# A new hand-written order for the first 26 slots of a linear attention with two feed-forward layers

## The chip, the cores and the metric

The kernel runs on one core of a Trainium2 chip. The core has five engines with an instruction list each: TensorE (PE, matrix products), VectorE (DVE), ScalarE (ACT), GpSimd (POOL) and SyncE (SP, which issues almost all transfers here). Each works its list strictly in order and waits at an instruction until what it needs is there. The metric is the device time of one execution in microseconds; the number quoted is the median of several runs.

## The reference

For 4 batches, 8 heads, 768 steps and head size 48, a state of 48 x 48 per head is carried along the steps; the result then goes through two feed-forward layers of width 2048 over 3072 tokens of 384 features.

```python
for t in range(S):
    cur = einsum('bhd,bhe->bhde', u[None] * k_t, v_t)
    y[:, :, t] = einsum('bhd,bhde->bhe', r_t, state + cur)
    state = w[None, :, :, None] * state + einsum('bhd,bhe->bhde', k_t, v_t)
h = x @ w_in1;  x = (max(h, 0) + alpha * min(h, 0)) @ w_out1
h = x @ w_in2;  x = (h * tanh(log1p(exp(h)))) @ w_out2
```

Weights are given as 64-bit floats, everything else as 32-bit floats.

## The kernel before

Tokens go in six blocks of 512 columns (128 steps of all four batches). A *slot* is one block with one of the 16 groups of 128 hidden features: slots 0 to 95 are the first layer (`mA_...`), and the second layer (`mB_...`) has as many behind them. Slot 2, slot 8 and so on below are first-layer slots of block 0 and block 1.

Every large product is taken as three with operands split in a high and a low part (`PASSES`), so a slot is nine products for `mA_h` (to the bank `h`, of which there are two in turn) and nine for `mA_out` (to the banks `acc`). Between them stand `mA_g` (ACT takes the negative part, DVE the weighted sum, L658 and L660), `mA_hi` (ACT) and `mA_lo` (DVE). Slots 0 and 1 are cut in halves of the columns and in passes: `mA_h 0 1 2` is slot 0, half 1, pass 2.

A weight group passes through `more_raw` (SP loads the raw words; three buffers in turn, a buffer is free again after that group's `w_join`), `w_scale` (ACT, two operations), `w_join` (DVE), `w_hi` (ACT) and `w_lo` (DVE). For groups 0 and 1 each of these is done in two halves.

Attention goes in *units*. Units 0 to 3 are the four batches' first 128 steps, each through `load_unit`, `m_first`, `prep_rk`, `c_first`, `preset_first`, `scores`, `masked`, `attend0`, `x_first`, `x_first_lo`, and then `prep_kn` and `states_first` for the state. Tables of decay powers (`tables`, `scale_Kn`, `table_Kn`, `seats`) and the constants `cst` (identity and mask) come before. From unit 4 on a unit is 64 steps of two batches: `load_unit`, `prep_pair`, `prep_c`, `prep_c2`, `prep_kn`, `preset`, `masked`, then `batch` (TensorE, which also holds the next unit's `scores` and takes one `h` bank), `t_decay`, `t_update`, and `x_parts`, which moves the result out of the banks and sets the `h` bank free.

The order is written out by hand. Each step has a name (its function and arguments) and `PLACES` gives the place at which it is issued; `run_plan` sorts all steps by place and issues them, so a step's place sets its order on every engine it uses, SP included. A step with the place `None` is left out. An entry `"?name": 1` moves that step to another engine, by `other()`:

```python
def other():
    return PLACES.get("?" + now[0], 0)
```

For `w_hi` that is POOL instead of ACT, for `w_lo`, `prep_pair`, `prep_rk` and `m_first` POOL instead of DVE, for `preset` one POOL operation instead of four of ACT, for `prep_c2` sixteen short ACT operations instead of one reduction on DVE, for `t_decay` four ACT operations instead of one of DVE.

`keep_warm` multiplies zeros into a bank that nobody reads, to keep TensorE at work where it would wait: five groups ahead of all steps, and those that `PLACES` gives a place.

Of the kernel before, what the change touches and what calls it, by code (L numbers as in the profile page):

```python
# [54 lines left out]
def more_state(u):  # L55
# [9 lines left out]
    "?preset 9 1": 1, "tables": 8.049, "keep_warm 3#######": 8.099, "scale_Kn": 8.149, "memset": 8.199,  # L65
    "load_unit 0": 8.249, "m_first 0": 8.299, "prep_rk 0": 8.349, "c_first 0": 8.399, "pad_v 0": 8.449,
    "load_unit 1": 8.499, "preset_first 0": 8.549, "dma_start": 8.599, "table_Kn 1": 8.649, "pad_v 1": 8.699,
    "m_first 1": 8.749, "prep_rk 1": 8.799, "load_unit 3": 8.849, "<lambda> 3": 8.899, "load_unit 2": 8.949,
    "load_k 2": 8.999, "<lambda> 0": 9.049, "scores 0": 9.099, "masked 0": 9.149, "m_first 3": 9.199, "seats": 9.249,
# [24 lines left out]
    "w_join (0,7)": 15.199, "w_scale (0,8)": 15.249, "dma_start##": 15.299, "w_join (0,8)": 15.349, "mA_hi 3": 15.399,  # L94
# [1017 lines left out]
```

## Time and profile before

| | us |
|---|---|
| runs (median 863.0) | 862.88, 863.0, 864.82 |
| the profiled execution, its time | 864.74 |
| the profiled execution, its span | 862.8 |
| TensorE busy | 854.3 |
| DVE busy | 629.9 |
| ACT busy | 612.3 |
| POOL busy | 115.1 |

The span is the time from the first to the last instruction of the profiled execution; its own time is a little longer. Busy times of engines overlap. An engine's idle time matters only where another engine, in the end TensorE, waits for it.

### The profile page before, as it was taken

What the parts mean: (1) busy time and instruction counts of PE and PEld (TensorE: products, weight loads), DVE (VectorE), ACT (ScalarE), POOL (GpSimd) and SP (SyncE); (2) the same over time, 40 slices, a digit from 0 to 9 for tenths busy, and PEclk for the clock granted to TensorE, in tenths of its full rate; (3) what the DMA queues carried; (4) which work ended last, traced back from release to release, by engine and by line L of the source; (5) the groups of instructions that cost most, each with busy time, mean ns of one, the idle gap of its engine ahead of it and who ended that gap; (6) DMA issues with size and microseconds to landing.
All of it is one profiled execution on the core that took longest, in us unless ns stands there. A gap on an engine that the chain in (4) does not pass through costs nothing.

```text
span 862.8 us, 16681 instructions
## 1 busy us (share of the span) xinstructions
PE 854.3 (99%) x6382; PEld 709.8 (82%) x6382; DVE 629.9 (73%) x969; ACT 612.3 (71%) x1170; POOL 115.1 (13%) x133
## 2 busy tenths in 40 slices
PE   9999999999999999999999999999999999999998
PEld 6887888888888888888888888888888888888897
DVE  8889776666656656444666887887887887887875
ACT  5987555445545445543556989989989998998886
POOL 5465641112211112100002000000000000000000
PEclk9999999999999999999999999999999999999999
DMA  9886734364255434223520300110110110100101
GB/s 347 260 247 179 223 99 133 96 206 135 84 163 162 147 85 171 66 65 120 172 78 15 111 1 1 32 43 1 30 45 1 29 47 0 30 9 1 28 10 38
DMA packets 65328, 79.95 MB, mean 93 GB/s; under 512 B 39648, under 2 KB 52448, under 8 KB 65248
## 3 DMA queue, kind: packets, MB, share of 16 engines
q1 hardware_dynamic: 64688, 78.78, 30.4%
q8 instruction: 50, 0.82, 0.4%
q14 instruction: 30, 0.25, 0.1%
q10 hardware_dynamic: 560, 0.10, 0.1%
HBM read 61.16 MB, written 15.73 MB: 89 GB/s over the span
## 4 chain that ended last, share of the span: by engine, by line
PE 92%; DVE 2%; ACT 2%; DMA 2%; issue 1%; POOL 0%; SPq 0%; DVEq 0%; ACTq 0%; POOLq 0%
PE h L269 43%; PE acc L690 21%; PE sc L817 8%; PE acc L817 8%; PE yt L817 4%; PE acc L815 2%; PE sc L501 1%; DMA nat<-in_nat 1%; PE h L532 1%; PE sc L815 1%; PE yt L553 1%; PE sc L546 1%; DMA cst<-in_consts 1%; PE yt L532 1%; ACT wrawr L216 0%
## 5 line engine op out<-in xcount | busy, mean ns | idle before, releaser
L269 PE MATMUL h<-x,w 128*128 128x512 f32 (+1 forms) x1746 | 415.5, 387 | 2.1 <-DVE x L190 1.9
L269 PEld LDWEIGHTS h<-x,w 128*128 128x128 f32 x1746 | 325.0, 188 | 69.7 <-issue 2.5
L690 PE MATMUL acc<-ghi,w 128*128 128x512 f32 x516 | 174.9, 394 | 0.0
L658 ACT ACTIVATE m<-h 128x512 f32<-128x512 f32 x96 | 57.1, 595 | 92.8 <-PE h L269 92.7
L660 DVE SCALAR_TENSOR_TENSOR g<-m,oma,h 128x512 f32<-128x512 f32 x96 | 71.6, 746 | 60.2 <-ACT m L658 59.2
L690 PEld LDWEIGHTS acc<-ghi,w 128*128 128x128 f32 x516 | 96.8, 188 | 21.3
L187 ACT ACTIVATE ghi<-g 128x512 fp32r<-128x512 f32 x86 | 54.2, 630 | 74.9 <-PE acc L690 48.0
L690 PE MATMUL acc<-glo,w 128*128 128x512 f32 x258 | 100.4, 389 | 0.0
L190 DVE TENSOR_TENSOR glo<-g,ghi 128x512 fp32r<-128x512 f32 x86 | 62.8, 730 | 51.5 <-ACT ghi L187 51.2
L754 DVE SCALAR_TENSOR_TENSOR a<-ghi,h 128x512 f32<-128x512 f32 x96 | 66.0, 687 | 38.5 <-ACT ghi L751 32.0
L754 DVE SCALAR_TENSOR_TENSOR g<-s,c 128x512 f32<-128x512 f32 x95 | 66.6, 701 | 22.5 <-ACT s L751 20.4
L762 ACT ACTIVATE m<-h 128x512 f32<-128x512 f32 x96 | 56.4, 588 | 35.6 <-PE h L269 35.6
L190 DVE TENSOR_TENSOR gloB<-g,ghiB 128x512 fp32r<-128x512 f32 x105 | 72.0, 685 | 7.1 <-ACT ghiB L187 7.1
L751 ACT ACTIVATE ghi<-m,biases 128x512 f32<-128x512 f32 x96 | 69.6, 725 | 3.2
L187 ACT ACTIVATE ghiB<-g 128x512 fp32r<-128x512 f32 x105 | 64.8, 617 | 9.1 <-PE acc L690 6.9
L751 ACT ACTIVATE glo<-ghi,biases 128x512 f32<-128x512 f32 x96 | 68.1, 709 | 0.1
L751 ACT ACTIVATE s<-glo,biases 128x512 f32<-128x512 f32 x96 | 68.1, 709 | 0.0
L751 ACT ACTIVATE s<-s,biases 128x512 f32<-128x512 f32 x96 | 68.0, 708 | 0.0
L817 PE MATMUL sc<-ghiB,w 128*128 128x512 f32 x192 | 66.9, 389 | 0.0
L754 DVE SCALAR_TENSOR_TENSOR b<-ghi,a 128x512 f32<-128x512 f32 x96 | 65.6, 684 | 0.1
L754 DVE SCALAR_TENSOR_TENSOR c<-glo,b 128x512 f32<-128x512 f32 x95 | 65.7, 691 | 0.0
L817 PE MATMUL acc<-ghiB,w 128*128 128x512 f32 x192 | 61.7, 389 | 0.0
(189 smaller groups left out, 1148.3 us busy)
## 6 DMA issues: line engine op xcount, KB each, us to landing
wrawr<-in_w SPq DMA_DIRECT2D x28, 768.0 KB, 5.3
nat<-in_nat SPq DMA_DIRECT2D x40, 288.0 KB, 4.4
w2d<-wj SPq DMA_DIRECT2D x16, 384.0 KB, 2.5
wraw<-w2d SPq DMA_DIRECT2D x16, 384.0 KB, 3.1
rk<-in_rkT SPq DMA_DIRECT2D x40, 128.0 KB, 3.1
x2d<-xo SPq DMA_DIRECT2D x6, 768.0 KB, 3.2
x<-x2d SPq DMA_DIRECT2D x6, 768.0 KB, 4.6
rk<-in_rkT SPq DMA_DIRECT2D x40, 96.0 KB, 2.8
```

Source lines behind the costliest of these rows:

```text
L187: act.activation(out=hi, in_=src, func=AF.Copy)
L190: eng.tensor_tensor(out=lo, in0=src, in1=hi.bitcast(F32), op=ALU.subtract)
L269: pe.matmul(h[:, n], w_in(layer, f, a, c), x[:, b, c, n], start=(k == 0), stop=(k == 3 * KC - 1))
L532: pe.matmul(y[i][64 * q:64 * q + 64, p * HC:(p + 1) * HC], T[ROWS[h], 2 * bp + i, k, :], pair[i][ROWS[h], 0, k, t], start=(r == 0 and not ...
L658: act.activation(out=m, in_=hA[s], func=AF.Relu, scale=-1.0)
L660: dve.scalar_tensor_tensor(out=g, in0=m, scalar=oma[:, f:f + 1], in1=hA.pop(s), op0=ALU.mult, op1=ALU.add)
L690: pe.matmul(acc[0][c], w_out(0, f, a)[:, c * 128:(c + 1) * 128], g[b], start=(f == 0 and k == 0), stop=(f == NF - 1 and k == 2))
L751: act.activation(out=out, in_=in_, func=AF.Square, scale=scale, bias=fin[bias])
L754: dve.scalar_tensor_tensor(out=out, in0=in0, scalar=scalar, in1=in1, op0=op0, op1=ALU.mult)
L762: act.activation(out=bnew("t", n), in_=v["h", n], func=AF.Tanh, scale=0.5)
L815: pe.matmul(acc[1][t][:, :DM], g[a][:, t * C:(t + 1) * C], w_out(1, f, b), **se)
L817: pe.matmul(acc[1][t], w_out(1, f, a)[:, t * 128:(t + 1) * 128], g[b], **se)
```

## The change

Only `PLACES` is changed: the places of all steps up to 26.599, the set of steps that go to another engine, and one group of zero products more that gets no place. From `mA_hi 22` on the order is the same. The core of the diff, with the lines that matter below (each side is a dictionary in the order of places; lines left out hold the same steps at other places):

```diff
-    "?w_lo (0,4)": 1, "?t_decay 4": 1, "?t_decay 9": 1, "?preset_first 1": 1, "?prep_c2 4": 1, "?t_decay 5": 1,
-    "?preset 6 0": 1, "?w_lo (0,12)": 1, "?t_decay 6": 1, "?w_hi (0,15)": 1, "?preset 8 0": 1, "?preset 8 1": 1,
-    "?prep_pair 10 1": 1, "?preset 9 0": 1, "?w_hi (0,1) 1": 1, "?preset 4 0": 1, "?m_first 2": 1, "?w_hi (0,3)": 1,
-    "?w_hi (0,4)": 1, "?prep_pair 6 1": 1, "?prep_pair 8 1": 1, "?preset 7 0": 1, "?preset 7 1": 1, "?w_lo (0,15)": 1,
-    "?preset 9 1": 1, "tables": 8.049, "keep_warm 3#######": 8.099, "scale_Kn": 8.149, "memset": 8.199,
-    "load_unit 0": 8.249, "m_first 0": 8.299, "prep_rk 0": 8.349, "c_first 0": 8.399, "pad_v 0": 8.449,
-    "load_unit 1": 8.499, "preset_first 0": 8.549, "dma_start": 8.599, "table_Kn 1": 8.649, "pad_v 1": 8.699,
...
-    "prep_rk 2": 9.799, "prep_rk 3": 9.849, "keep_warm 3##########": 9.899, "load_k 1": 9.949, "scores 1": 9.999,
...
-    "w_scale (0,1) 0": 10.299, "keep_warm 3#########": 10.349, "w_join (0,0) 0": 10.399, "w_join (0,0) 1": 10.449,
...
-    "w_lo (0,8)": 16.249, "load_unit 5": 16.299, "prep_c 5": 16.349, "mA_h 6": 16.399, "w_hi (0,7)": 16.449,
...
-    "masked 4": 17.249, "mA_out 5": 17.299, "batch 4": 17.349, "mA_hi 6": 17.399, "mA_lo 6": 17.449, "mA_out 6": 17.499,
-    "prep_kn 5": 17.549, "w_scale (0,10)": 17.599, "load_unit 7": 17.649, "w_hi (0,9)": 17.699, "w_join (0,10)": 17.749,
-    "mA_h 8": 17.799, "mA_g 7": 17.849, "t_decay 4": 17.899, "w_lo (0,9)": 17.949, "mA_hi 7": 17.999, "mA_lo 7": 18.049,
-    "mA_out 7": 18.099, "prep_pair 6 0": 18.149, "x_parts 4": 18.199, "preset 5 0": 18.249, "preset 5 1": 18.299,
-    "masked 5": 18.349, "mA_g 8": 18.399, "w_hi (0,10)": 18.449, "t_update 4": 18.499, "w_scale (0,11)": 18.549,
...
+    "?w_lo (0,4)": 1, "?preset_first 1": 1, "?t_decay 5": 1, "?t_decay 6": 1, "?w_hi (0,15)": 1, "?preset 8 1": 1,
+    "?prep_pair 10 1": 1, "?w_lo (0,15)": 1, "?m_first 3": 1, "?w_lo (0,1) 1": 1, "?w_lo (0,1) 0": 1, "?w_hi (0,3)": 1,
+    "?preset 4 0": 1, "?w_hi (0,9)": 1, "?t_decay 4": 1, "?prep_c2 5": 1, "?preset 5 0": 1, "?preset 5 1": 1,
+    "?w_hi (0,10)": 1, "?w_hi (0,13)": 1, "?prep_c2 8": 1, "?prep_pair 10 0": 1, "?preset 10 0": 1, "tables": 8.099,
+    "load_unit 0": 8.149, "<lambda> 0": 8.199, "load_unit 3": 8.249, "m_first 0": 8.299, "scale_Kn": 8.349,
+    "prep_rk 0": 8.399, "c_first 0": 8.449, "preset_first 0": 8.499, "dma_start": 8.549, "table_Kn 1": 8.599,
+    "load_unit 1": 8.649, "m_first 1": 8.699, "scores 0": 8.749, "masked 0": 8.799, "dma_start#": 8.849,
+    "tensor_scalar": 8.899, "seats": 8.949, "pad_v 1": 8.999, "load_unit 2": 9.049, "<lambda> 2": 9.099,
...
+    "m_first 2": 9.449, "pad_v 2": 9.499, "more_raw 2": 9.549, "more_raw 1": 9.599, "keep_warm 3#######": 9.649,
...
+    "keep_warm 3##########": 10.449, "w_scale (0,1) 0": 10.499, "w_join (0,0) 0": 10.549, "w_join (0,0) 1": 10.599,
...
+    "mA_hi 0": 13.599, "w_hi (0,1) 1": 13.649, "more_raw 8": 13.699, "more_raw 9": 13.749, "mA_lo 0": 13.799,
...
+    "mA_hi 2": 14.599, "mA_lo 2": 14.649, "mA_h 3": 14.699, "prep_c 4": 14.749, "mA_g 3": 14.799, "load_unit 5": 14.849,
...
+    "mA_g 6": 17.149, "preset 4 1": 17.199, "masked 4": 17.249, "w_hi (0,8)": 17.299, "load_unit 7": 17.349,
+    "w_lo (0,8)": 17.399, "mA_hi 6": 17.449, "mA_lo 6": 17.499, "more_raw 15": 17.549, "more_raw 16": 17.599,
+    "mA_g 7": 17.649, "prep_kn 4": 17.699, "w_lo (0,9)": 17.749, "batch 4": 17.799, "x_parts 4": 17.849,
+    "prep_c 6": 17.899, "w_scale (0,10)": 17.949, "prep_pair 6 0": 17.999, "w_join (0,10)": 18.049,
+    "w_hi (0,10)": 18.099, "mA_hi 7": 18.149, "mA_lo 7": 18.199, "mA_h 8": 18.249, "mA_h 9": 18.299, "mA_g 8": 18.349,
+    "t_decay 4": 18.399, "t_update 4": 18.449, "prep_c2 6": 18.499, "preset 5 0": 18.549, "preset 5 1": 18.599,
+    "prep_kn 5": 18.649, "w_scale (0,11)": 18.699, "masked 5": 18.749, "mA_hi 8": 18.799, "mA_lo 8": 18.849,
...
```

On SP the loads go, before: unit 0, unit 1, `cst`, unit 3, unit 2, ..., weights 0 to 6, unit 4, weights 7 to 9, `ubt`, weight 10, unit 5, unit 6, weights 11 and 12, unit 7, ... After: unit 0, unit 3, `cst`, unit 1, `al`, unit 2, ..., weights 0 to 6, `ubt`, unit 4, weights 7 and 8, unit 5, weight 9, unit 6, weights 10 to 13, unit 7, weights 14 and 15, unit 8, ...

On TensorE, from slot 2 on, before: `mA_h 2`, `mA_out 0`, `mA_h 3`, `mA_out 1`, `mA_h 4`, `mA_h 5`, `mA_out 2`, `mA_out 3`, `mA_h 6`, `scores 4`, `mA_out 4`, `mA_h 7`, `mA_out 5`, `batch 4`, `mA_out 6`, `mA_h 8`, `mA_out 7`, and, behind `x_parts 4`, `mA_h 9` and on. After: `mA_h 2`, `mA_out 0`, `mA_h 3`, `mA_out 1`, `mA_h 4`, `mA_out 2`, `mA_out 3`, `mA_h 5`, `mA_h 6`, `mA_out 4`, `mA_h 7`, `scores 4`, `mA_out 5`, `batch 4`, `mA_h 8`, `mA_h 9`, `mA_out 6`, `mA_out 7`, `mA_out 8`, `mA_h 10`, `batch 5`, and on.

## Rows read from the trace of the kernel before

**Rows 1.** The page, part 1: busy us (share of the span) and instructions.

```profile
PE 854.3 (99%) x6382; PEld 709.8 (82%) x6382; DVE 629.9 (73%) x969; ACT 612.3 (71%) x1170; POOL 115.1 (13%) x133
```

**Rows 2.** Busy time by stretch: from:to, length, engines, granted clock, DMA share, GB/s.

```profile
8.54:31.31 22.77, 22.36 (x380) 19.48 (x380) 20.80 (x27) 19.51 (x49) 13.33 (x16) 1.00 0.96 362
31.31:67.97 36.66, 34.42 (x299) 27.55 (x296) 31.60 (x38) 31.25 (x74) 18.68 (x16) 1.00 0.85 245
67.97:95.00 27.03, 27.03 (x475) 22.31 (x476) 24.35 (x41) 20.20 (x46) 15.98 (x14) 1.00 0.69 206
95.00:220.00 125.00, 125.00 (x1383) 103.32 (x1382) 79.42 (x127) 61.75 (x151) 33.62 (x39) 1.00 0.47 138
220.00:858.00 638.00, 637.21 (x3826) 531.87 (x3825) 467.65 (x728) 476.83 (x847) 29.87 (x38) 1.00 0.20 58
```

**Rows 3.** Timeline of TensorE at 67.97: start us, us, instructions merged, [idle before <-releaser].

```profile
67.97 2.33 PE L269 MATMUL h<-x,w 128*128 128x512 f32 x9 [1.87 <-DVE x L190]
```

**Rows 4.** Timeline of TensorE: the first zero products, and `scores 4`.

```profile
1.30 6.08 PE L641 MATMUL acc<-ghi 128*128 128x384 f32 x12 [1.30 <-POOL ghi L943]
...
50.42 0.69 PE L501 MATMUL sc<-rk 48*64 48x64 f32 x32
```

**Rows 5.** The chain that ended last, in order of time: start us, us, what.

```profile
3.15 5.26 DMA cst<-in_consts
...
45.37 8.54 DMA nat<-in_nat
...
82.63 2.04 PE acc L690 x9
...
86.58 2.28 PE h L269 x9
```

**Rows 6.** Groups of DVE instructions, 30 to 68 us: count, busy us, mean ns, idle before.

```profile
L225 DVE SCALAR_TENSOR_TENSOR wj<-wrawr 128x768 uint32<-128x768 uint32 x7 | 7.9, 1136 | 0.8 <-ACT wrawr L217 0.7
L190 DVE TENSOR_TENSOR glo<-g,ghi 128x512 fp32r<-128x512 f32 x8 | 6.5, 819 | 2.3 <-ACT ghi L187 2.3
L190 DVE TENSOR_TENSOR w<-wj,w 128x768 fp32r<-128x768 f32 x6 | 6.1, 1043 | 0.0
L660 DVE SCALAR_TENSOR_TENSOR g<-m,oma,h 128x512 f32<-128x512 f32 x8 | 6.0, 744 | 1.6 <-ACT m L658 1.3
L419 DVE TENSOR_TENSOR rk<-rk,RKs 112x1024 f32<-112x1024 f32 x3 | 5.9, 1950 | 0.0
L505 DVE COPY_PREDICATED Ah<-cst,sc 128x512 f32<-128x512 uint32 x2 | 1.5, 737 | 0.0
L454 DVE TENSOR_REDUCE cc<-nat 128x8 f32<-128x384 f32 x1 | 0.6, 558 | 0.9 <-POOL nat L446 0.9
```

**Rows 7.** Timelines of DVE and POOL near 63 us.

```profile
63.61 3.42 DVE L419 TENSOR_TENSOR rk<-rk,RKs 112x1024 f32<-112x1024 f32 x1
66.95 0.21 DVE L190 TENSOR_TENSOR y<-yt,y 112x64 fp32r<-112x64 f32 x1
...
63.10 2.85 POOL L419 TENSOR_TENSOR rk<-rk,RKs 112x1024 f32<-112x1024 f32 x1
```

**Rows 8.** Timeline of POOL: two casts of a weight group, one `preset`.

```profile
26.90 0.83 POOL L236 CAST w<-wj 128x768 fp32r<-128x768 f32 x1 [3.08 <-PE acc L581]
...
48.99 1.04 POOL L466 TENSOR_TENSOR Ah<-cst,cc 128x256 f32<-128x256 f32 x1 [1.12 <-ACT nat L452]
...
91.50 1.96 POOL L236 CAST w<-wj 128x768 fp32r<-128x768 f32 x1
```

**Rows 9.** Timeline of SP: issue us, length of the issue.

```profile
35.49 0.33 SPq L207 DMA_DIRECT2D wrawr<-in_w  x1
...
44.85 1.11 SPq L324 DMA_DIRECT2D nat<-in_nat  x2
```

**Rows 10.** Transfers up to 75 us: count, KB each, median us from issue to landing.

```profile
w14u<-in_rkT SPq DMA_DIRECT2D x1, 512.0 KB, 6.0
...
al<-in_alphaT SPq DMA_DIRECT2D x1, 8.0 KB, 8.5
```

More of the change, by code (lines that the diff above doesn't have):

```diff
@@ L60 @@
 PLACES = {
[4 rows of a table removed]
-    "?preset 9 1": 1, "tables": 8.049, "keep_warm 3#######": 8.099, "scale_Kn": 8.149, "memset": 8.199,
-    "load_unit 0": 8.249, "m_first 0": 8.299, "prep_rk 0": 8.349, "c_first 0": 8.399, "pad_v 0": 8.449,
-    "load_unit 1": 8.499, "preset_first 0": 8.549, "dma_start": 8.599, "table_Kn 1": 8.649, "pad_v 1": 8.699,
-    "m_first 1": 8.749, "prep_rk 1": 8.799, "load_unit 3": 8.849, "<lambda> 3": 8.899, "load_unit 2": 8.949,
-    "load_k 2": 8.999, "<lambda> 0": 9.049, "scores 0": 9.099, "masked 0": 9.149, "m_first 3": 9.199, "seats": 9.249,
[24 rows of a table removed]
-    "w_join (0,7)": 15.199, "w_scale (0,8)": 15.249, "dma_start##": 15.299, "w_join (0,8)": 15.349, "mA_hi 3": 15.399,
[63 rows of a table removed]
[4 rows of a table added]
+    "load_unit 0": 8.149, "<lambda> 0": 8.199, "load_unit 3": 8.249, "m_first 0": 8.299, "scale_Kn": 8.349,
+    "prep_rk 0": 8.399, "c_first 0": 8.449, "preset_first 0": 8.499, "dma_start": 8.549, "table_Kn 1": 8.599,
+    "load_unit 1": 8.649, "m_first 1": 8.699, "scores 0": 8.749, "masked 0": 8.799, "dma_start#": 8.849,
+    "tensor_scalar": 8.899, "seats": 8.949, "pad_v 1": 8.999, "load_unit 2": 9.049, "<lambda> 2": 9.099,
[15 rows of a table added]
+    "dma_start##": 12.849, "half_tables": 12.899, "w_lo (0,2)": 12.949, "load_unit 4": 12.999, "w_scale (0,6)": 13.049,
[9 rows of a table added]
+    "tables_seat": 15.399, "more_raw 10": 15.449, "mA_h 4": 15.499, "mA_g 4": 15.549, "w_scale (0,7)": 15.599,
[63 rows of a table added]
 }
```

155 rows, old and new, of the table PLACES are left out of this document.

## The prediction

> **What bounds the kernel now.** I read the page first, for the share of each engine: TensorE is busy for 99% of the span [rows 1]. A new order on the other engines can therefore only give back what TensorE waits, and the next view has to say where it waits. That is the table of busy time by stretch [rows 2]; its cuts are the landing of `cst` (8.54 us), the start of slot 2 (31.31) and the end of the longest wait (67.97). Between the first two TensorE is idle for 22.77 - 22.36 = 0.41 us, up to 67.97 for 36.66 - 34.42 = 2.24, up to 220 for nothing, and up to 858 for 638.00 - 637.21 = 0.79, where the order is not changed. The granted clock is 1.00 in all five stretches, so no time is lost to it. The timeline of TensorE, third, shows the largest piece: 1.87 us before the nine products of slot 9, for DVE's subtraction in `x_parts` [rows 3]. Fourth comes the chain that ended last, read backwards from that place: it goes back over DVE and POOL to `nat` of unit 5, which took 8.54 us to land from 45.37 on [rows 5]. Before `cst` has landed the order on TensorE has nothing to do but zero products.
>
> So the most that the change can give back is 0.41 + 2.24 = 2.65 us, unless TensorE gets less to do. From slot 2 on that is fixed: nine products take 2.04 us [rows 5], and their number is the same.
>
> **The zero products.** Before, six groups stand at the head (12 instructions, 6.08 us [rows 4]) and two behind `cst`. After, five stand at the head, because the group placed at 8.099 moves behind `seats`, and two again behind `cst`. So the group that is left out comes off the head only. There TensorE waits for `cst` in any case: its load was issued at 3.15 and landed 5.26 later [rows 5], and it stays sixth on SP's list behind loads of the same sizes. Gain 0. If the clock fell for want of the group, the bound is half of the head's own length, 3.0 us; I take 0, since the clock read 1.00 in the stretch with the 1.87 us wait, too.
>
> **The order up to slot 2.** TensorE's instructions behind `cst` are the same ones, so slot 2 can start at 8.54 + 22.36 = 30.90 if nothing waits: 0.41 gained. DVE was busy for 20.80 of the 22.77 us and hands two half `w_lo` to POOL (half of 1.043 each [rows 6]), so it fits in 22.36. New in the way is `tensor_scalar`, which moves from place 106 to 16 of the list: ACT then waits for `al`, ninth on SP's list. With the sixth issued at 3.15 it is issued near 4.7, one each 0.5 us. It lands 6.0 to 8.5 us later, by the load that stood near that place and by its own [rows 10]: 10.7 to 13.2. Behind it ACT has the copies of `seats`, ready when TensorE has done `table_Kn 1`, `scores 0` and `seats`, near 11.0, and `pad_v 0`, which the first attention matmul needs. The cost is 0 to 2.2; I take 0, because 6.0 is the row of a load two places further up, with no weights ahead of it either, while the 8.5 was queued behind weights.
>
> **The loads.** Unit 5's `nat` is issued at 44.85 before, behind four weight loads; after, it stands right behind `more_raw 9`, whose buffer comes free with a join. The load in that place went out at 35.49 [rows 9]. So it goes out some 9 us earlier and lands, even with its 8.54 us, near 45. The chain that the wait came from (`prep_c`, `prep_c2`, `masked 4`) is then not late: `masked 4` is wanted at the end of `scores 4`, near 54. `load_unit 7` goes behind `more_raw 14`, which waits for `w_join 10` (near 62); with 8.5 it lands by 71, and its batch comes near 89 (13 x 2.04 and two batches of 2.15 behind slot 8's start, below). `load_unit 8` stands behind three more weight loads, again with over ten us in hand. Cost 0.
>
> **Slots 2 to 8.** From 30.90 TensorE has six `mA_h` and six `mA_out` (12 x 2.04), `scores 4` (0.69 [rows 4]) and `batch 4`. A batch is the time between the end of the rows at 82.63 and the start at 86.58, 1.91, and 0.24 by which the nine products behind it are longer: 2.15 [rows 5]. So slot 8 is wanted at 58.2. Its bank needs the sum `mA_g 7`. Behind `mA_g 0` (done when slot 2 starts, since slot 2 uses its bank) DVE has up to there, at the means of [rows 6]: 7 sums at 0.744, 5 `w_lo` at 1.043, 7 `mA_lo` at 0.819, 6 joins at 1.136, 2 `prep_pair` at (3 x 1.950 - 3.42) / 2 = 1.21, one reduction 0.56 and one `masked` 0.74. That is 26.7 in the 27.3 us from 30.90 to 58.2: it fits, with 0.6 over. The 0.37 us of short waits that [rows 2] hold beside the 1.87 go with it.
>
> **Slot 9 and `mA_out 8`.** Slot 9 needs the bank that `x_parts 4` leaves; after, it stands directly behind `batch 4`, and `prep_pair 6 0` behind it instead of ahead of it. The subtractions took from 66.95 to 67.97 [rows 2, 7]; with half as much again for ACT's copies, an estimate from the same row, they end at 59.7, and slot 9 is wanted at 60.2. So the 1.87 goes. Then DVE does `prep_pair 6 0`, `w_join 10` (62.0), `mA_lo 7`, `mA_g 8`, `t_update 4`, `masked 5` and `mA_lo 8`: 65.9 at the same means, the addition taken as 0.74. `mA_out 8` wants that at 58.2 + 4 x 2.04 = 66.4. But `masked 5` now waits for both halves of `preset 5`, which move to POOL behind `w_hi 10`, which moves to POOL too. From the join, a cast of 0.83 to 1.96 and two presets of 1.04 [rows 8] end at 64.9 to 66.0, and `masked 5` with `mA_lo 8` (1.56) at 66.5 to 67.6. A wait of 0.1 to 1.2 is new; the lower bound is none. I take 0.4, near the cast of 0.83, for the hand-overs between.
>
> **POOL beside DVE.** The multiplication `prep_pair 6 0` took 3.42 on DVE, 2.2 over its 1.21, while POOL ran the other half for 2.85 [rows 7]. POOL began at 63.10 and ended at 65.95; 1.21 more is 67.16, within 0.15 of DVE's end. So DVE stood still until POOL was through. Here this second half goes back to DVE, but `w_hi 9`, `w_hi 10` and both `preset 5` come to POOL. The Trainium skill says it as a rule (SBUF — State Buffer, "Who interferes with whom"): a DVE instruction with two SBUF inputs and a GpSimd instruction that reads SBUF exclude one another for the whole instruction. The trace agrees here; whether it holds for casts and presets, no row shows. What it would do is the last rival.
>
> **After slot 10.** TensorE waits for nothing from 67.97 to 220, and DVE is busy for 24.35 of 27.03, then for 79.42 of 125 [rows 2]. What is moved there (casts 13, presets 6 to 10, `prep_c2 8`, `prep_pair 8 1` and `10 0`, `t_decay 9`) has that as cover. Without it each would cost its own length, at most 2.0 for a cast. Cost 0.
>
> **Sum.** Against the profiled execution: 864.74 - 0.41 - 2.24 + 0.4 = 862.5 us. That execution is the slow end of the runs shown (862.88, 863.0, 864.82). The two groups are 1.85 apart, which is the size of the 1.87 wait: I read it as a wait that some runs have and others don't, so the sum for the changed kernel stands only 0.5 below the median before.
>
> **Rivals.** First, the wait is in every run, and what differs is time around the span (864.74 - 862.8 = 1.94 here). Then the median loses all of it: 863.0 - 2.65 + 0.4 = 860.8. Only the coincidence of 1.85 and 1.87 speaks against it. Second, the wait moves to `mA_out 8` at its upper end: 862.1 + 1.2 = 863.3; for it speaks the cast of 1.96. Third, the clock falls at the head: 862.5 + 3.0 = 865.5, and no row shows it. Fourth, slower: POOL's new work stops DVE ahead of slot 8 and `mA_out 8`. The two casts and two presets are up to 2 x 1.96 + 2 x 1.04 = 6.0 us. At the share lost in [rows 7], 2.2 of 2.85, DVE loses 4.6, has 0.6 to spare, and TensorE waits 4.0: 862.1 + 4.0 = 866.1. It decides (over 865.6) once DVE loses 4.1 of the 6.0. Against it: over [rows 6] the joins, `mA_lo`, `w_lo` and `prep_pair` are long by some 5 us in all beside 18.68 us of POOL [rows 2], about a quarter; and a quarter of the 3.1 that POOL gains net is 0.8, which leaves 0.2 of wait.
>
> **How the numbers follow.** Forecast 0.58, between 861.6 and 863.0; first rival 0.17; second 0.14; third 0.02; fourth 0.09. A measurement of this kernel can tell about 0.3%, 2.6 us, from no change: under 860.4 lies a third of the first rival, 0.06; over 865.6 the fourth, 0.09; the rest, 0.85, is no change. The range from 860.4 to 864.5 takes in the forecast, the second rival and two thirds of the first, and leaves out 0.17.
>
> **What would show it.** Right: slot 2 starts near 30.9, slot 8 near 58, unit 5's `nat` is issued before 40, and the wait of `mA_h` for `x_parts` is gone. `mA_out 8` waiting for `mA_lo 8` with POOL's presets ahead of it would be the new term. Wrong: ACT idle on `al` up to 13, a clock under 1.00 before 31, joins and subtractions on DVE of 2 us and more beside POOL, or any wait of TensorE between 68 and 110.

## The result and the profile after

Six runs of the changed kernel took 866.38 to 870.47 us, median 868.23; six of the kernel before, in turn with them, had a median of 862.94. The ratio is 1.0056 (95% interval 1.0037 to 1.0075): slower by 0.56%, 5.3 us. The forecast of 862.5 and its range up to 864.5 were wrong, and in sign.

The page of the changed kernel, part 1, answers to [rows 1]:

```profile
PE 856.3 (99%) x6380; PEld 711.5 (82%) x6380; DVE 632.2 (73%) x969; ACT 615.1 (71%) x1193; POOL 110.7 (13%) x131
```

TensorE has two instructions less and is busy 2.0 us longer. That it is busy longer with less to do already points at its clock. Busy time by stretch (columns as in [rows 2]; the first three lines have the cuts used there, the last two cut the first stretch around a wait):

```profile
8.54:31.31 22.77, 20.22 (x323) 17.10 (x320) 18.89 (x20) 16.42 (x44) 12.98 (x16) 0.93 0.96 365
31.31:67.97 36.66, 34.81 (x339) 28.59 (x338) 32.16 (x40) 29.80 (x65) 16.31 (x15) 1.00 0.69 206
67.97:95.00 27.03, 27.03 (x358) 22.16 (x357) 24.64 (x40) 22.11 (x58) 11.69 (x13) 1.00 0.69 216
...
20.50:26.13 5.63, 3.17 (x61) 2.56 (x59) 5.63 (x6) 5.29 (x10) 4.70 (x5) 1.00 1.01 417
26.13:30.48 4.35, 4.35 (x59) 3.92 (x59) 2.98 (x4) 0.97 (x2) 2.89 (x4) 0.61 0.82 214
```

Up to 31.31 TensorE stood idle for 22.77 - 20.22 = 2.55 us, where it was 0.41, and the granted clock is 0.93 there. It fell to 0.61 for 4.35 us, right behind the wait: for most of that stretch the engine ran at the lower of its two levels, 1.2 instead of 2.4 GHz. The timeline of TensorE shows wait and fall, and two more waits later:

```profile
23.23 0.62 PE L269 MATMUL h<-x,w 128*128 128x256 f32 x3
26.13 0.62 PE L269 MATMUL h<-x,w 128*128 128x256 f32 x3 [2.29 <-DVE x L190]
26.68 0.71 PE L581 MATMUL acc<-w13u 128*48 128x48 f32 x16
27.17 0.85 PE L581 MATMUL acc<-w15u 128*48 128x48 f32 x16
27.81 2.74 PE L516 MATMUL acc<-A,w15u 128*64 128x128 f32 x24
...
65.03 4.39 PE L269 MATMUL h<-x,w 128*128 128x512 f32 x18 [1.41 <-DVE g L660]
...
101.69 0.51 PE L690 MATMUL acc<-glo,w 128*128 128x512 f32 x1 [0.98 <-DVE glo L190]
```

The 24 attention products at 27.81 take 2.74 us; the same 24 take 1.53 in the kernel before. There DVE did its four half `w_lo` in one row while POOL stood still, 0.49 us each:

```profile
24.49 1.53 PE L516 MATMUL acc<-A,w15u 128*64 128x128 f32 x24
...
23.92 1.95 DVE L190 TENSOR_TENSOR w<-wj,w 128x384 fp32r<-128x384 f32 x4
```

The wait of 2.29 is that of `mA_h 0 0 1` for `x_first_lo 1`. What DVE did ahead of that subtraction in the changed kernel, and POOL at the same time:

```profile
20.57 0.54 DVE L190 TENSOR_TENSOR x<-h,x 128x384 fp32r<-128x384 f32 x1
21.03 0.69 DVE L190 TENSOR_TENSOR w<-wj,w 128x384 fp32r<-128x384 f32 x1
21.64 3.97 DVE L190 TENSOR_TENSOR w<-wj,w 128x384 fp32r<-128x384 f32 x1
25.53 0.54 DVE L190 TENSOR_TENSOR x<-h,x 128x384 fp32r<-128x384 f32 x1
```

```profile
20.30 1.00 POOL L458 TENSOR_TENSOR w13u<-w13u,Kn 128x384 f32<-128x384 f32 x1
21.25 0.96 POOL L890 MEMSET T<- 112x1024 f32 x1
22.17 1.08 POOL L482 TENSOR_SCALAR_AFFINE_SELECT A<-cc 128x1024 f32<-128x1024 f32 x1
23.22 1.01 POOL L458 TENSOR_TENSOR w15u<-w15u,Kn 128x384 f32<-128x384 f32 x1
24.19 1.00 POOL L190 TENSOR_TENSOR w<-wj,w 128x384 fp32r<-128x384 f32 x1
```

The second of DVE's two half `w_lo` took 3.97 us, where the first took 0.69. It ended at 25.61, 0.42 behind the end of POOL's row at 25.19. The first had ended at 21.72, 0.42 behind the end of POOL's operation at 21.30 and in the middle of the memset. `x_first_lo 1` stands behind the second, and TensorE behind that.

Slot 2 starts at 35.22 instead of 30.90. Of these 4.32 us, 2.55 are idle time, nearly all of it the wait of 2.29; in the other 1.77 TensorE is busy longer, by the clock. The sum then closes on the profiled execution's 869.18: 862.5 forecast, + 4.32 for slot 2, + 1.78 for two waits of `mA_h` for `mA_g` (0.37 and 1.41), + 0.98 at `mA_out 13`, - 0.4 for a wait of `mA_out 8` that didn't come, is 869.18.

### The profile page after: what moved, and what is told of

It reads as the page before. It is cut to its first block, busy times and chain, and to the rows that moved or that the text cites. A ratio compares the mean times of both kernels' runs of the same rounds, so it can differ in the third digit from the quotient of the medians.

```text
span 867.2 us, 16698 instructions
## 1 busy us (share of the span) xinstructions
PE 856.3 (99%) x6380; PEld 711.5 (82%) x6380; DVE 632.2 (73%) x969; ACT 615.1 (71%) x1193; POOL 110.7 (13%) x131
## 4 chain that ended last, share of the span: by engine, by line
PE 92%; DMA 3%; DVE 2%; ACT 2%; issue 1%; SPq 0%; DVEq 0%; POOL 0%; ACTq 0%; POOLq 0%
PE h L269 43%; PE acc L690 22%; PE sc L817 8%; PE acc L817 8%; PE yt L817 4%; PE acc L815 3%; DMA wrawr<-in_w 1%; PE sc L815 1%; DMA w5r<-in_w 1%; PE sc L501 1%; PE h L532 1%; PE yt L553 1%; PE sc L546 1%; DMA w10u<-in_rkT 1%; PE yt L532 1%
```

## The experiments

Experiments that change a few places show the entries of `PLACES` against the changed kernel's. All do the full computation. Each ratio is against the kernel before, run on the same chip beside it; that kernel's own median went from 862.44 to 863.70 from chip to chip, so a difference between medians of two experiments can be off by about a microsecond.

**a_start_before and b_start_after: which half of the order loses?**

```diff
 a: order and engines of the kernel before up to mA_h 2, the changed kernel's from there
 b: the changed kernel's up to mA_h 2, those of the kernel before from there
```

> Order and engines of before up to slot 2, those of after from there on. If the loss is made in the start (theory: DVE's second half w_lo stands still behind POOL for 3.97 us, TensorE waits 2.29, the clock then reads 0.61 for 4.35 us, slot 2 starts 3.9 us late), slot 2 starts at 31.3 again, no stretch reads under 1.00, and the time is 863.5 to 864.5. If the loss is made behind slot 2 (rival: the third transfer of raw weights late, prep_c2 5 on ACT, the wait near 101), it stays at 866 or more.

> The other half: order and engines of after up to slot 2, those of before from there on. Theory (loss in the start): slot 2 starts near 35.2, the time is 866 to 867.5. Rival (loss behind slot 2): 863 to 864.5.

Kernel a: 865.51 (864.48 to 866.4), ratio 1.0035 (1.0022 to 1.0048). Kernel b: 869.31 (866.92 to 869.98), ratio 1.0082 (1.0065 to 1.0099). Neither is where it was expected: a is 1.0 over the theory's range and 0.5 under the rival's bound, b is 1.8 over the theory's. By the larger ratio the start carries more of the loss, and a shows that the rest isn't free: its clock reads 1.00 in all stretches, but it has a wait of 1.01 at `mA_out 13`, like the changed kernel. Two of its waits stand in neither kernel and so probably come from the seam:

```profile
45.68 0.50 PE L687 MATMUL acc<-glo,w 128*128 128x512 f32 x1 [0.62 <-DVE glo L187]
49.06 3.94 PE L266 MATMUL h<-x,w 128*128 128x512 f32 x16 [0.78 <-DVE w L187]
```

Kernel b, too, has two such waits (0.71 and 0.95 us for weights, at 45.28 and 46.95). It gave more than was asked: its profiled execution has the same wait of 2.29, yet the clock behind it is whole (the timeline, then the busy time by stretch):

```profile
26.24 0.62 PE L266 MATMUL h<-x,w 128*128 128x256 f32 x3 [2.29 <-DVE x L187]
```

```profile
26.24:31.00 4.76, 4.76 (x76) 4.44 (x77) 4.19 (x6) 2.88 (x5) 2.99 (x4) 1.00 0.85 226
```

That execution took 866.92 at a mean clock of 1.000; the other three took 869.26 to 869.98 at 0.996 to 0.998. So the wait and the clock are two costs, and the second doesn't come with every execution. It is some 2.4 us by these times; no trace of the three is there to show where their clock fell.

**c_xlo_first: the two `w_lo` off the way.**

```diff
-"x_first_lo 1": 11.849, "masked 3": 11.899
+"x_first_lo 1": 11.674, "masked 3": 11.684   # ahead of both w_lo (0,0) on DVE
```

> After, with x_first_lo 1 and masked 3 issued on DVE ahead of the two half w_lo instead of behind them; POOL, ACT and TensorE keep their lists. Theory: DVE's two w_lo still stand behind POOL, but nobody waits for them: the wait of 2.29 goes to under 0.4, the clock stays at 1.00, slot 2 starts at 30.8 to 31.5, the time falls by 3.5 to 4.5 to about 864. Rival (the start is late because of ACT: x_first 1 and the weights' halves come too late): mA_h 0 0 1 still waits over 1 us.

863.9 (863.54 to 865.95), ratio 1.0016 (1.0007 to 1.0025): by moving two steps some 4 us of the 5.3 are back (4.3 by the two medians; against the kernel before beside it, 5.3 became 1.5). Neither the wait of 2.29 nor the fall of the clock is there, and slots 2 to 8 wait for nothing:

```profile
31.31:70.00 38.69, 38.67 (x321) 31.62 (x320) 35.30 (x46) 33.43 (x75) 20.12 (x19) 1.00 0.76 231
```

The waits of 0.37 and 1.41 that the changed kernel has there are gone as well (below). Slot 2 starts at 32.07, later than the 30.8 to 31.5 expected. Left are 0.55 at 29.49, where `mA_h 1 1 0` waits for `x_first_lo 3`, and 0.99 at `mA_out 13`.

**e_pool_gap: fewer POOL operations beside the same `w_lo`.**

```diff
-"half_tables": 12.899, "prep_kn 3": 11.649, "states_first 2": 12.249
+"half_tables": 11.905, "prep_kn 3": 11.91, "states_first 2": 12.32   # prep_kn 3 later on POOL
```

> After, with prep_kn 3 on POOL put behind half_tables, which waits for masked 3, so that POOL has two operations less next to DVE's w_lo, and states_first 2 put behind attend0 3. DVE keeps its list. Theory (DVE's second w_lo stands still as long as POOL has operations in a row that read SBUF): the w_lo ends near 23.4 instead of 25.6, the wait of TensorE shrinks from 2.29 to under 0.5, the clock stays at 1.00, the time falls by 2.5 to 4. Rival (the w_lo is late for its own data, w_hi of ACT or the transfer of the weights): it ends near 25.5 as before and the time stays at 868.

867.44 (866.85 to 868.79), ratio 1.006 (1.0045 to 1.0075). The two `w_lo` together take 2.64 us here, and 4.58 in the changed kernel (21.03 to 25.61); POOL's row now ends at 23.42, and again DVE is through 0.41 behind that:

```profile
21.19 2.64 DVE L192 TENSOR_TENSOR w<-wj,w 128x384 fp32r<-128x384 f32 x2
```

The first wait shrinks from 2.29 to 0.33 and the clock stays at 1.00, but the delayed steps hand it on:

```profile
24.36 0.62 PE L271 MATMUL h<-x,w 128*128 128x256 f32 x3 [0.33 <-DVE x L192]
...
28.84 0.56 PE L583 MATMUL acc<-w15u 128*48 128x48 f32 x16 [1.33 <-POOL w15u L460]
```

TensorE also waits 0.65 and 0.38 in the start, and 0.87 at 79.54 for nothing that the profile shows. So the `w_lo` is as long as POOL's row, as the theory has it, but the fall of 2.5 to 4 us in time did not come: as a repair the move is worthless.

**g_zeros_in_gap: the same wait, with zeros in it.**

```diff
+"keep_warm 3#########": 12.101, "keep_warm 3###########": 12.111, "keep_warm 3############": 12.121
 # between mA_h 0 0 0 (12.099) and mA_h 0 0 1 (12.149)
```

> After, with three groups of zero products (some 2.3 us) put on TensorE between mA_h 0 0 0 and mA_h 0 0 1, where it waits 2.29; all other lists stay. Theory (part of the loss is that the clock falls behind that wait: 4.35 us at a mean of 0.61): the products behind the gap start at the same time near 26.1, no stretch reads under 1.00, slot 2 starts 1.5 to 2 us earlier, the time falls by 1.5 to 2.5 to about 866. Rival (attend0 3 and states_first are long there for their own reasons, the lists beside them): no change, 868.

865.34 (864.35 to 872.73), ratio 1.0049 (1.0021 to 1.0078), by medians 2.9 under the changed kernel. The ratio does not show a gain, since one execution of 872.73, at a mean clock of 0.995 and without a trace, is in it; the other four read 1.000. What the trace shows is clearer. DVE is as late as there (`mA_h 0 0 1` starts at 26.43), and only the clock differs: timeline and stretch behind it.

```profile
23.95 2.10 PE L643 MATMUL acc<-ghi 128*128 128x384 f32 x6
26.43 0.62 PE L271 MATMUL h<-x,w 128*128 128x256 f32 x3 [0.37 <-DVE x L192]
```

```profile
26.43:31.00 4.57, 4.57 (x74) 4.25 (x75) 4.00 (x6) 2.70 (x5) 2.99 (x4) 1.00 0.81 210
```

By rows, the time from `mA_h 0 0 1`'s start to the row behind the attention products is 1.6 us shorter at the full clock (26.24 to 28.98 in b, 26.13 to 30.48 in the changed kernel: 2.74 and 4.35). That is the price of the fall alone; five runs that reach from 864.35 to 872.73 don't give it better.

**k_memset_last: the same POOL row, the memset at its end.** It ran twice, the second time as k_again.

```diff
-"memset": 11.299, "w_lo (0,1) 0": 12.399
+"w_lo (0,1) 0": 11.66, "memset": 11.67
```

> After, with POOL's memset of T moved behind w_lo (0,1) 0, so that POOL does prep_kn 2, preset_first 3, prep_kn 3, half a w_lo and then the memset in a row. If DVE's second half w_lo stands still only beside POOL operations that read SBUF, it ends some 0.4 us behind POOL's half w_lo, near 24.7, and TensorE's wait is near 1.3. If it stands still beside the memset too, it ends some 0.4 us behind the memset, near 25.6, and the wait stays at 2.3.

> The kernel of k_memset_last, which had one run only (863.75): if DVE's short second w_lo (1.44 us) and the full clock are there in each execution, the median is 863.2 to 864.5; if it was a lucky execution, it is near the kernel after, 866 and more.

One run of 863.75, then 863.88 (863.56 to 866.31), ratio 1.001 (1.0 to 1.0021). This is in neither branch of the first expectation: POOL has as much to do, but DVE now gets in after one of POOL's operations, and the two of POOL's that were 1.08 and 1.01 are longer. DVE, then POOL:

```profile
21.05 2.05 DVE L192 TENSOR_TENSOR w<-wj,w 128x384 fp32r<-128x384 f32 x2
```

```profile
21.27 1.42 POOL L484 TENSOR_SCALAR_AFFINE_SELECT A<-cc 128x1024 f32<-128x1024 f32 x1
22.66 1.31 POOL L460 TENSOR_TENSOR w15u<-w15u,Kn 128x384 f32<-128x384 f32 x1
```

So it is not the amount of POOL's work that cost 3.97 us but who gets the turn.

**f_lo13_first and h_three_moves: the waits that are left in c.**

```diff
 both: as c, and
-"mA_lo 13": 22.599
+"mA_lo 13": 22.52        # ahead of x_parts 7 on DVE
 h alone:
-"x_first_lo 3": 12.649
+"x_first_lo 3": 12.575
```

> The run with x_first_lo 1 and masked 3 ahead of the two w_lo, and besides mA_lo 13 issued ahead of x_parts 7 instead of behind it. Theory (the wait of 1.0 at mA_out 13 comes from x_parts 7 standing ahead of mA_lo 13 on DVE, behind the end of batch 7): the wait is gone and the time falls by 0.8 to 1.2 against that run (863.9), to about 862.9. Rival (it comes from POOL's w_lo (0,15) beside it, 1.84 us): mA_lo 13 is still long and a wait over 0.5 stays.

> The run with mA_lo 13 first, and besides x_first_lo 3 issued on DVE ahead of w_join (0,1) 1 instead of behind it. Theory (0.55 at mA_h 1 1 0 is DVE's x_first_lo 3 behind a join that POOL's prep_kn 0 lengthens to 1.37): that wait goes, the time falls by a further 0.3 to 0.6, to 862.2 to 862.6, which is the time of before (862.4). Rival (the rest of the loss is in later slots): it stays at 862.9 or over.

f: 863.59 (862.5 to 868.25), ratio 1.0011 (0.9997 to 1.0025); h: 863.81 (863.33 to 866.48), ratio 1.0015 (1.0005 to 1.0025). Neither is clear of c (1.0016), and both miss the times that were expected (862.9, and 862.2 to 862.6). In f the 0.99 at `mA_out 13` is gone, and 0.39 turns up at `mA_out 15`. In h the 0.55 of `x_first_lo 3` is gone, too, and two others stand there:

```profile
31.91 2.34 PE L271 MATMUL h<-x,w 128*128 128x512 f32 x9 [0.77 <-DVE g L662]
...
106.23 0.50 PE L692 MATMUL acc<-glo,w 128*128 128x512 f32 x1 [0.82 <-DVE glo L192]
```

The first is slot 2 behind `mA_g 0`: ACT sits in `w_scale (0,6)` ahead of it, for weights that have not landed. The second is `mA_lo 15`, 2.69 us long on DVE beside `prep_pair 10 0`, which the change gave to POOL. The third move gained nothing.

**l_all_waits and m_no_zeros: all named waits at once; then one zero product group less.**

```diff
 both: as k_memset_last, and
-"mA_lo 13": 22.599, "w_scale (0,6)": 13.049, "?prep_pair 10 0": 1
+"mA_lo 13": 22.52, "w_scale (0,6)": 13.41
 m alone:
-"keep_warm 3##########": 10.449
+"keep_warm 3##########": None
```

> The kernel after with every wait of TensorE that the runs named taken out at once: POOL's memset behind its half w_lo (as in k_memset_last), mA_lo 13 ahead of x_parts 7 on DVE (as in f_lo13_first), w_scale (0,6) behind mA_g 0 on ACT (its load of the weights came too late, and mA_g 0 stood behind it), prep_pair 10 0 back on DVE. Theory (the loss is the sum of these waits): k_memset_last's 863.75 less its 0.99 at mA_out 13 and its 0.71 at mA_h 2, 862.0, no wait over 0.4 of TensorE between 8.5 and 110, clock 1.00 in every stretch; that is the kernel before within 0.3 per cent. Rival (each move only hands the wait on, as the third move in h_three_moves did): 863.5 to 864.5, with a new wait of 0.5 or more named in the trace.

> The kernel of l_all_waits with one zero product group less (one stays instead of two). Theory A (TensorE is full between 8.5 and slot 2, so a group there costs its own time): 0.6 to 0.8 us below l_all_waits. Theory B (the prediction's: the group fills a hole in which TensorE waits for its data anyway): the same as l_all_waits within 0.4. If the clock falls by it, 2 us and more above.

l: 862.81 (861.92 to 864.76), ratio 0.9993 (0.9984 to 1.0002). The whole loss is back, and the kernel stands where the kernel before does. The theory's 862.0 was 0.8 too low and one wait over 0.4 is left, 0.59 ahead of slot 8, in a profiled execution of 864.15. In its stretches, the start is full and 1.45 us are idle in the second:

```profile
8.54:31.31 22.77, 22.68 (x381) 19.71 (x382) 19.62 (x24) 18.65 (x47) 14.08 (x17) 1.00 0.97 370
31.31:67.97 36.66, 35.21 (x298) 27.47 (x297) 31.13 (x41) 30.25 (x68) 19.61 (x18) 1.00 0.79 221
```

l makes four moves on top of each other; what each is worth alone was not run.

m: 865.93 (864.29 to 868.92), ratio 1.0032 (1.0021 to 1.0044), 3.1 above l on the same chip. Both theories fail; the last sentence of the expectation came true. Shortly behind the place of the group, TensorE waits 0.80 us for DVE, and two microseconds later the clock falls (timeline, then stretches):

```profile
17.42 1.10 PE L503 MATMUL sc<-w12u 48*64 48x64 f32 x32 [0.80 <-DVE A L507]
18.46 1.05 PE L439 MATMUL acc<-ut,g 112*128 112x2 f32 x8
19.44 2.35 PE L518 MATMUL h<-A,w11u 128*64 128x128 f32 x24
```

```profile
17.42:19.44 2.02, 2.02 (x40) 1.83 (x41) 2.02 (x4) 2.02 (x7) 0.90 (x2) 1.00 1.03 405
19.44:23.95 4.51, 4.51 (x53) 4.33 (x55) 2.82 (x5) 2.88 (x7) 3.40 (x5) 0.62 1.02 425
```

Not all of the 3.1 is this: `mA_g 7` is waited for 1.19 us there (0.59 in l), and 1.02 are new at 80.64.

**n_third_group: the group that the change left out, put back.**

```diff
-"keep_warm 3#########": None
+"keep_warm 3#########": 10.16     # behind attend0 0
```

> The kernel after with the zero product group that the change took out put back, behind attend0 0 (between 13.7 and 14.7, as in the kernel before it stands between attend0 0 and c_first); nothing else changed. Theory (the loss comes from the 2.29 wait on x_first_lo 1 that stands between DVE's two half w_lo, and that wait and the clock behind it have nothing to do with the group): the same as the kernel after within 0.7, 867.5 to 869, the wait shorter by up to 0.75 since TensorE reaches mA_h 0 0 1 that much later, and the clock still under 1.00 behind it. Rival (the group less is what lets the clock fall, as one less did in m_no_zeros): 865 to 866, clock 1.00 in the stretch behind the wait. Third: the group stands on the path at the start and costs its 0.75: about 869.

867.01 (865.63 to 870.03), ratio 1.0046 (1.003 to 1.0062). That is 1.2 under the changed kernel, 0.5 under the theory's interval and 1.0 over the rival's, and the two ratios' intervals overlap. The trace decides: the wait is there, 0.37 shorter since TensorE arrives later, and the clock falls. It need not fall each time, though: one of the seven executions, the shortest at 865.63, has a mean clock of 1.000, where all six of the changed kernel read 0.997 or 0.998. Nor is n's shorter time the group's doing: its slot 2 starts no earlier (35.35 against 35.22), and most of the 2.17 us between the two profiled executions are the 1.78 that the changed kernel waits for `mA_g` and n does not (below, the loads).

```profile
26.30 0.62 PE L271 MATMUL h<-x,w 128*128 128x256 f32 x3 [1.92 <-DVE x L192]
```

```profile
26.00:31.00 5.00, 4.70 (x62) 4.37 (x63) 3.27 (x5) 1.24 (x3) 2.97 (x4) 0.66 0.78 211
```

## Why the prediction was wrong, point by point

Of the signs of being wrong that the prediction named, three came: a clock under 1.00 before 31, a subtraction of over 2 us on DVE beside POOL, and a wait between 68 and 110.

**The order up to slot 2: the step that failed.** It said that DVE "was busy for 20.80 of the 22.77 us and hands two half `w_lo` to POOL", "so it fits in 22.36", cost 0. The total is right and says nothing about the order: in c, with all that work done on time, DVE is busy for 19.47 of the 23.36 us from `cst` to slot 2. Two other half `w_lo` stand on DVE ahead of `x_first_lo 1`, whose turn is pressing. They got no price of their own (half a `w_lo` counts as half of 1.043), and POOL's four operations beside them were never laid next to them. One took 3.97, TensorE waited 2.29, and the clock fell behind it. c shows the place (some 4 of 5.3 us back), e and k the mechanism, and g that the clock is a cost of its own.

**POOL beside DVE** was seen, and looked for in the wrong place: the fourth rival puts it ahead of slot 8, from presets and casts. The prediction asked for it where new work came to POOL, not where DVE's new order put its own work beside what POOL had all along. Ahead of slot 8 it did come, smaller and from another operation (below, the loads). On its size the prediction read from [rows 7] that DVE stood still until POOL was through; with a row of four operations that came true: the 0.42 us that DVE ends behind the row are about the operation's own length (1.95 / 4 = 0.49 in the kernel before). The Trainium skill (SBUF — State Buffer, "Who interferes with whom") says that whichever engine issues first keeps the other out for its whole instruction. The trace agrees that DVE stands still, but DVE lost three instructions in a row in the changed kernel and one in k_memset_last. The page also says that a GpSimd instruction which only writes does not keep DVE out. The trace agrees for the first half `w_lo`, which ended at 21.72 while the memset ran from 21.25 to 22.21. The second started at 21.64, 0.53 us ahead of POOL's next operation, which is about its own length, and did not get through; by the rule of who issues first it should have kept that operation out. No run here shows why it didn't.

**The clock.** The third rival had it at 0.02, "since the clock read 1.00 in the stretch with the 1.87 us wait, too". One wait that it survived was no such evidence. It fell behind 2.29 in the changed kernel, 1.92 in n and 0.80 in m, and stayed up behind 2.29 in one execution of b. In f, too, two of ten executions (864.42 and 868.25) read 0.998, though the profiled one has no wait over 0.54 before 31; they have no trace. Of the bound of 3.0, 1.6 to 1.8 shows in the rows.

**The zero products.** Gain 0 held: n, with the group put back, has the same wait and the same fall. But a group is not worth nothing: m loses 3.1 for one. The rival was hung on the head of the kernel; the fall comes further back. (That TensorE has nothing but zero products to do ahead of `cst` was not exact: eight short products of `c_first` stand there, 0.95 us from 7.22. Nothing hangs on it.)

**`tensor_scalar`** cost 0, as taken: `al` landed 5.1 us after its issue, and ACT was idle on it for 0.28, out of TensorE's way.

**The loads and slots 2 to 8.** Unit 5's `nat` was issued at 40.27, not at 35.5, and took 11.6 us instead of 8.54. That was still hidden: c has no wait there, and in the changed kernel the chain that ended last at slot 8 does not go through this load but through that of weight group 9 (start, us, what; lines between left out):

```profile
46.68 8.82 DMA wrawr<-in_w
...
57.74 1.80 ACT nat L452 x16
...
62.71 1.42 DVE glo L190
...
64.23 0.76 DVE g L660
```

Weight group 9 lands at 55.5, and on ACT its `w_scale` stands ahead of `prep_c2 5`, and both ahead of the negative part that `mA_g 7` needs. ACT stood idle for 2.36 us on the load. The 1.42 of `mA_lo 6`, which is 0.68 in c and n, is DVE beside POOL's `prep_c 6`: about half of the wait of 1.41. So the fourth rival's mechanism is there ahead of slot 8, with some 0.7 us instead of 4.0.

A late start alone doesn't make this wait. Slot 2 starts at 32.07 in c, which has no such wait, and at 33.89 in g and 32.74 in m, which have it (1.40 and 1.19). But n, with 35.35 the latest of all, has none. It issued the load at 46.80 and used it at 53.20, with ACT not idle ahead of that:

```profile
53.20 0.91 ACT L218 ACTIVATE wrawr<-wrawr 128x768 f32<-128x768 f32 x1
```

TensorE is busy for all of 31 to 95 in n. So the wait also takes a load that is slow in that execution: 8.82 us in the changed kernel, at most 6.4 in n with the same order of loads. Why it is slow was not tried.

**Slot 9 and `mA_out 8`.** Right: `mA_h 8` and `mA_h 9` run as one row of 18 from 65.03 with no wait for `x_parts`, so the 1.87 is gone. The 0.4 for `mA_out 8` was too much: 67.97 to 95 has no wait.

**After slot 10.** "Cost 0" was wrong by 0.98. The cover was judged by DVE's share, 24.35 of 27.03, again a total. `mA_lo 13` stands behind `x_parts 7` on DVE and beside a `w_lo` of POOL, and takes 1.91 where [rows 6] have 0.819.

**The first rival** (the wait of 1.87 in every run) stays open. Of 82 executions of the kernel before, 55 took 862.08 to 863.24 and 27 took 863.58 to 865.38. That fits a wait that some have and others lack, as the prediction read it, but no trace of one without it was taken. Against that reading, l has such a group, too (864.15 and 864.76, the other nine up to 863.01), and its profiled execution of 864.15 has no wait for `x_parts`. If the reading holds, the change had little to win: 0.5 against the median.

Open is why DVE loses every turn with POOL's memset at the head of the row, and what besides a wait's length decides whether the clock falls.

## What to carry to other kernels

When an order is changed, don't compare an engine's busy total with the length of a stretch. Take the instruction that the bound engine waits for next, list what stands ahead of it on its engine, and price each at what runs beside it: a two-input DVE operation beside a row of POOL operations, at worst, by the end of that row. A wait of TensorE can have a second price, the clock behind it, here some 1.7 us, which doesn't come in every execution; zero products can be worth that, even where they fill a hole (l against m). And a wait that is taken away uncovers the next, so only the sum of all repairs (here l: back to the kernel before, and no further) tells what an order was worth.

## What the runs showed of the hardware that was not expected

- A DVE subtraction of half a weight group took 3.97 us beside POOL's row, where four of them took 1.95 in the kernel before with POOL idle; in the changed kernel, e, k_memset_last, l and n it ended 0.41 to 0.42 us behind the end of a POOL operation.
- The same four operations in another order on POOL (memset last) cost DVE one turn instead of three, and lengthened two of POOL's, by 0.34 and 0.30 us.
- TensorE's clock fell to 0.61 to 0.66 for 4 to 5 us behind waits of 0.80, 1.92 and 2.29 us, and did not fall behind one of 1.87 and one of 2.29.
- The same load of a weight group, issued in the same order of loads, landed after 8.82 us in the changed kernel and after at most 6.4 in n.
